# Four 64x64 tiles a slot, and an output projection in two pieces, in an attention and feed-forward kernel

## The chip, the core and the metric

The kernel runs on one core of one Trainium2 chip. The metric is the device time of one execution in microseconds (us); smaller is better. The time before is a median over three runs.

## What is computed

Inputs are q, k, v of shape (8 batches, 12 heads, 448 positions, 64) and the weights of a gated feed-forward layer, model width 768, hidden width 1536. Cut to what matters:

```python
scores = np.matmul(q, k.transpose(0, 1, 3, 2)) / np.sqrt(64)
attn = np.maximum(scores, 0.0) ** 2 / 448
x = np.matmul(attn, v)              # heads side by side: (8 * 448, 768)
xn = x / np.sqrt(np.mean(x * x, axis=-1, keepdims=True) + 1e-06) * rms_g
g = xn @ w_gate
out = (g / (1 + np.exp(-g)) * (xn @ w_val)) @ w_out
```

The matrix products run in bf16 and accumulate in fp32.

## The kernel before

**Two streams of work.** Attention of batch b + 1 is laid between the feed-forward products of batch b. `attention(b)` returns a list of units. For each pair of heads `j` and each block `c` of 128 keys there is one `scores` unit (line 212): two matmuls, one per head of the pair, each with 64 rows of contraction (the head size) and 128 output columns. `rectify` (lines 200, 202 and 205) takes the maximum with zero on ScalarE or VectorE into an SBUF tile `r`, and VectorE squares it. `attend` (line 258) multiplies the squares with v: seven groups of four matmuls with 64 rows and 64 columns, and between them one group of four from `rest_scores` (line 227), for the keys that are left over. Batches 0 and 1 get their transposed q and k from TensorE (line 177), the others by DMA.

**The feed-forward products.** A `Group` is one accumulation: for gate and value 6 blocks of 128 rows into a PSUM tile `psP` of 128x448, for the output projection 12 blocks into `psO`, and `norm_sums` with 6 blocks into `psSS`, which sums the squares of x for the norm. All are issued at line 380. Every block is cut into its lower and upper 64 rows, which are the two row halves of the array. `Stream.step` fills one slot: it picks a group `lead` for the lower half and another group `follow` for the upper half, and issues one matmul of each, 64 rows by 128 columns. A group so passes the lower half first with all its blocks, and the upper half later with the same blocks.

**The rules of picking.** `pick` lets a group go on until a multiple of six blocks, then takes the first open group that is `ready`, and for the lower half a new one from the list if none is. A group may change halves only when it has rested for `APART = 2` slots. On the change, a `nop` on TensorE's queue waits for the group's last matmul in the other half. A `Piece` (a part of the output projection) stops at half of its blocks until its siblings of the same 128 tokens are there too.

**PSUM.** `ps_m` has four banks, for all groups of the stream and the transposes. A new group begins only when a bank has been read out by its consumer: `silu` on ScalarE (line 451) for the gate, `hidden` on VectorE (line 456) for the value, `store` on ScalarE (line 490) for the output, the square root on ScalarE (line 420) for the norm. `ps_s` has two double banks, for scores and attention.

**The norm.** When `psSS` of batch b + 1 is complete, ScalarE takes the square root (with a table load on either side), VectorE the reciprocal (line 424), and then six multiplications, one for each 128 columns of the model width, give `xn` (line 427). The first product of batch b + 1 waits for these.

**The order.** All is issued in the order of the program; the loop at its end spreads the attention units over the first 82% of a batch's slots by an estimated cost. Before the loop, `attention(0)`, `norm(0)` and the first three products of batch 0 run by themselves.

Of the kernel before, what the change touches and what calls it, by code (L numbers as in the profile page):

```python
# [20 lines left out]
def kernel(  # L21
# [11 lines left out]
    nc = tc.nc  # L33
    P = nc.NUM_PARTITIONS
    B, H, S, D = q.shape
    T, DM = out.shape
# [27 lines left out]
    qkT = {}  # L64
# [3 lines left out]
    def load(nm, b, h0=0, h1=H):  # L68
        runs = nm == "v" or b < PE_T
        n, w = (PC, NCH) if nm == "q" else (P, UH)  # L70
        if (nm, b) not in ld:
            shape = [n, H, w * D] if runs else [n, w, H * D]
            ld[nm, b] = ldpool.tile(shape, BF16, name=nm + "b", tag=nm + "b")
            if nm == "k" and runs:
                nc.vector.memset(ld[nm, b][D:, :, (UH - 1) * D :], 0.0)
        t = ld[nm, b]
        src = src_of[nm][b, h0:h1]
        if nm == "q":
            parts = [(slice(0, PC), PC, 0, NCH)]
        else:  # L80
            parts = [(slice(0, D), D, 0, UH), (slice(D, P), D, UH if nm == "k" else UH - 1, U)]
        for prt, n, u0, u1 in parts:
            if runs:
                nc.gpsimd.dma_start(  # L84
                    out=t[prt, h0:h1, : (u1 - u0) * D],
                    in_=src.rearrange("h (p u) d -> p h (u d)", p=n)[:, :, u0 * D : u1 * D],
                )
            else:
                to = t[prt].rearrange("p u (h d) -> p u h d", d=D)
                rows = src.rearrange("h (p u) d -> p u h d", p=n)  # L90
                step = u1 - u0 if nm == "q" else 1
                for u in range(u0, u1, step):
                    nc.gpsimd.dma_start(  # L93
                        out=to[:, u - u0 : u - u0 + step, h0:h1, :], in_=rows[:, u : u + step]
                    )
# [4 lines left out]
    def transpose_dma(b):  # L100
        new_qkT(b)
        for c in range(UH):
            n = P if c < UH - 1 else D
            nc.sync.dma_start_transpose(
                out=qkT[b][:, :, 0, c * P : c * P + n], in_=ld["k", b][:n, c, :]
            )
        for c in range(NCH):
            nc.sync.dma_start_transpose(
                out=qkT[b][:, :, 1, c * PC : (c + 1) * PC], in_=ld["q", b][:, c, :]
            )  # L110
# [55 lines left out]
    behind = mybir.DependencyInfo(mybir.DependencyClass.Sync, mybir.DependencyReason.DATA)  # L166
# [30 lines left out]
    def rectify(b, j, c, psS):  # L197
        r = apool.tile([P, 2, S], BF16, name="r", tag="r")
        if relu_on(b, j, c) == "dve":
            nc.vector.tensor_relu(out=r[:], in_=psS[:, :, :S])  # L200
        else:
            nc.scalar.activation(out=r[:], in_=psS[:, :, :S], func=ACT.Relu)  # L202
        eng = nc.gpsimd if square_on(b, j, c) == "pool" else nc.vector
        flush()
        pending.append(lambda: eng.tensor_tensor(out=r[:], in0=r[:], in1=r[:], op=ALU.mult))  # L205
        rsq[b, j, c] = r

    def scores(b, j, c):
        psS = ps_s.tile([P, 2, 512], FP32, name="psS", tag="psS")
        for hh in range(2):  # L210
            prt = slice(hh * D, (hh + 1) * D)
            nc.tensor.matmul(  # L212
                out=psS[:, hh, :S],
                lhsT=qkT[b][prt, j, 0, c * P : (c + 1) * P],
                rhs=qkT[b][prt, j, 1, :],
                start=True,
                stop=True,
            )
        rectify(b, j, c, psS)

    def rest_scores(b, j):
# [59 lines left out]
    def attention(b):  # L281
        units = []

        def add(cost, *fns):
            units.append((cost, lambda: [f() for f in fns]))

        if b < PE_T:
            add(0.4, lambda: transposes(b, 0))
            add(0.4, lambda: transposes(b, 1))
            add(0.3, lambda: rectify(b, 0, UH - 1, rest_scores(b, 0)))  # L290
        for j in range(HP):
            for c in range(UH - 1):
                if c == 2 and j in (2, 4):
                    add(1.6, lambda j=j: attend(b, j - 2, (b, j)))
                add(0.3, lambda j=j, c=c: scores(b, j, c))
                if c == 1 and b < PE_T and j + 2 < HP:
                    add(0.4, lambda j=j: transposes(b, j + 2))
                if b == 0:
                    add(0.3, lambda: keep_busy(1))
        add(0.1, flush)  # L300
        add(1.6, lambda: attend(b, HP - 2, (b + 1, 0) if PE_T <= b + 1 < B else None), flush)
        return units
# [3 lines left out]
    class Stream:  # L306
# [28 lines left out]
        def step(self):  # L335
            if not (self.todo or self.open):
                return False
            lead = self.pick(0, None)
            follow = self.pick(1, lead)
            for half, g in ((0, lead), (1, follow)):  # L340
                if g is not None:
                    g.emit(half)
            self.at = [lead, follow]
            for g in self.open:
                g.rest += 1
            if follow is not None and follow.count[1] == follow.n:
                self.open.remove(follow)
                follow.done(follow.ps)
            return True
# [7 lines left out]
    class Group:  # L357
# [14 lines left out]
        def begin(self):  # L372
            self.ps = ps_m.tile([P, 512], FP32, name=self.name, tag="mm")

        def emit(self, half):
            i = self.count[half]
            prt = slice(half * D, (half + 1) * D)
            if self.last not in (None, half):
                tc.add_manual_dep(nc.tensor.nop().ins, self.mm.name, behind)
            mm = nc.tensor.matmul(  # L380
                out=self.ps[:, : self.w], lhsT=self.lhsT(i)[prt], rhs=self.rhs(i)[prt],
                start=(half == 0 and i == 0), stop=(half == 1 and i == self.n - 1),
            )
            self.count[half] += 1
            self.last, self.rest = half, 0
            self.mm = mm.ins

    class Piece(Group):

# [81 lines left out]

    osts = {}

    OW = DM // 3

    def outproj(i, t):
        trio = []
        for o in range(0, DM, OW):
            Piece(
                trio, FT, OW, lambda fk: hTs[i][:, fk, t * P : (t + 1) * P],  # L480
                lambda fk, o=o: wo_sb[:, fk, o : o + OW],
                lambda ps, o=o: store(i, t, o, OW, ps), "psO",
            )
        return trio

    def store(i, t, o, w, ps):
        if (i, t) not in osts:
            osts[i, t] = [opool.tile([P, DM], FP32, name="ost", tag="ost"), 0]
        ost = osts[i, t][0]
        nc.scalar.copy(out=ost[:, o : o + w], in_=ps[:, :w])  # L490
        osts[i, t][1] += w
        if osts[i, t][1] == DM:
            g, end = t * P, (t + 1) * P
            while g < end:
                n = min(end, (g // PC + 1) * PC) - g
                b, c, p0 = 2 * i + g // S, g % S // PC, g % PC
                rows = out[b * S : (b + 1) * S, :].rearrange("(p u) m -> p u m", u=NCH)
                nc.sync.dma_start(
                    out=rows[p0 : p0 + n, c, :], in_=ost[g - t * P : g - t * P + n, :]
                )  # L500
                g += n
# [21 lines left out]
    for b in range(B):  # L523
# [9 lines left out]
        if b + 2 < B:  # L533
            for nm in ("q", "k", "v"):
                load(nm, b + 2)
            side.insert(len(side) // 2, (0, lambda b=b: transpose_dma(b + 2)))
        cost = {KT: S / 2.4 + 2.5, FT: OW / 2.4 + 2.5}
        total = sum(g.n * cost[g.n] for g in groups)
# [41 lines left out]
```

## Time and profile before

| | |
|---|---|
| median of three runs | 468.2 us (466.82, 468.2, 469.97) |
| span of the profiled execution | 466.5 us, 12798 instructions |
| the profiled execution's own time | given by the page as its span alone |
| TensorE matmul busy | 453.6 us, 97% of the span, 5722 matmuls |
| TensorE weight load busy | 292.8 us, 63% |
| VectorE busy | 274.0 us, 59% |
| ScalarE busy | 234.9 us, 50% |
| GpSimd busy | 80.6 us, 17% |
| mean granted TensorE clock | 0.982 |

Engines are named PE (TensorE matmul), PEld (TensorE weight load), DVE (VectorE), ACT (ScalarE) and POOL (GpSimd). A group line of the page reads: line of the kernel, engine, operation, output <- inputs, rows*columns of the array tile and shapes, count, then busy time and mean duration of one in ns. A timeline line reads: start in us, length in us, engine, line, operation, shapes, count; matmuls that overlap are merged into one line. "64*128" is an array tile of 64 rows and 128 columns. A matmul's duration goes from its first column to its last result, and the next one on the same tile starts before that; the pace is read from starts.

### The profile page before, as it was taken

What the parts mean: (1) busy time and instruction counts of PE and PEld (TensorE: products, weight loads), DVE (VectorE), ACT (ScalarE), POOL (GpSimd) and SP (SyncE); (2) the same over time, 40 slices, a digit from 0 to 9 for tenths busy, and PEclk for the clock granted to TensorE, in tenths of its full rate; (3) what the DMA queues carried; (4) which work ended last, traced back from release to release, by engine and by line L of the source; (5) the groups of instructions that cost most, each with busy time, mean ns of one, the idle gap of its engine ahead of it and who ended that gap; (6) DMA issues with size and microseconds to landing.
All of it is one profiled execution on the core that took longest, in us unless ns stands there. A gap on an engine that the chain in (4) does not pass through costs nothing.

```text
span 466.5 us, 12798 instructions
## 1 busy us (share of the span) xinstructions
PE 453.6 (97%) x5722; PEld 292.8 (63%) x5722; DVE 274.0 (59%) x403; ACT 234.9 (50%) x360; POOL 80.6 (17%) x97
## 2 busy tenths in 40 slices
PE   6989999999999999999999999999999999999995
PEld 3434655676666766676666766676667766676674
DVE  1676378866663867576566657576656677332200
ACT  1682246665645655375445755465535764532221
POOL 8438211571007000340007000100000000000000
PEclk8698999999999999999999999999999999999998
DMA  9999999799907970299209960438002200020013
GB/s 106 194 204 199 206 173 162 80 204 165 127 3 107 214 124 2 23 200 146 44 1 124 211 109 1 58 82 135 20 1 54 85 2 1 2 84 20 1 42 95
DMA packets 130758, 44.47 MB, mean 95 GB/s; under 512 B 102928, under 2 KB 127120, under 8 KB 130704
## 3 DMA queue, kind: packets, MB, share of 16 engines
q0 software_dynamic: 91648, 24.39, 54.1%
q1 hardware_dynamic: 39056, 19.28, 20.5%
q8 instruction: 44, 0.72, 0.6%
q14 instruction: 10, 0.08, 0.0%
HBM read 48.76 MB, written 11.01 MB: 128 GB/s over the span
## 4 chain that ended last, share of the span: by engine, by line
PE 91%; DVE 3%; ACT 2%; DMA 1%; POOL 1%; issue 1%; POOLq 0%
PE psP L380 47%; PE psO L380 23%; PE psAV L258 8%; PE psS L212 6%; PE psSS L380 2%; ACT r L202 2%; PE psB L140 1%; PE psT L177 1%; PE psS L227 1%; DMA kb<-in_k_dram 1%; DVE xn L427 1%; PE psP L441 1%; DVE r L200 1%; DVE r L205 1%; DVE rstd L424 1%
## 5 line engine op out<-in xcount | busy, mean ns | idle before, releaser
L380 PE MATMUL psP<-xn,wv_sb 64*128 64x448 bf16 x1140 | 229.0, 349 | 0.0
L380 PE MATMUL psP<-xn,wg_sb 64*128 64x448 bf16 x1128 | 227.8, 349 | 0.1
L380 PE MATMUL psO<-wo_sb,hT 64*128 64x256 bf16 x2016 | 139.6, 271 | 0.0
L202 ACT ACTIVATE r<-psS 128x896 bf16<-128x896 f32 x123 | 111.1, 918 | 47.5 <-PE psS L212 46.8
L380 PEld LDWEIGHTS <-wv_sb 64*128 64x128 bf16 x1140 | 96.1, 94 | 41.5 <-issue 4.3
L380 PEld LDWEIGHTS <-hT 64*128 64x128 bf16 x2016 | 101.1, 94 | 33.0 <-issue 2.9
L380 PEld LDWEIGHTS <-wg_sb 64*128 64x128 bf16 x1128 | 94.3, 94 | 35.6 <-issue 1.3
L205 DVE TENSOR_TENSOR r<-r 128x896 bf16<-128x896 bf16 x165 | 100.9, 628 | 16.3 <-ACT r L202 15.6
L456 DVE TENSOR_TENSOR hT<-sil,psP 128x448 bf16<-128x448 bf16 x96 | 59.5, 620 | 79.7 <-PE psP L380 52.4
L451 ACT ACTIVATE sil<-psP 128x448 bf16<-128x448 f32 x96 | 51.9, 542 | 74.7 <-PE psP L380 68.8
L200 DVE TENSOR_SCALAR r<-psS 128x896 bf16<-128x896 f32 x45 | 49.1, 1090 | 31.7 <-PE psS L227 24.2
L212 PE MATMUL psS<-qkT 64*128 64x448 bf16 x288 | 59.3, 358 | 1.9 <-DVE r L200 1.2
L490 ACT COPY ost<-psO 128x256 f32<-128x256 f32 x84 | 30.5, 372 | 43.5 <-PE psO L380 39.6
L276 ACT ACTIVATE xT<-psAV 128x896 bf16<-128x896 f32 x24 | 22.0, 917 | 54.4 <-PE psAV L258 50.1
L258 PE MATMUL psAV<-r,vb 64*64 64x448 bf16 x672 | 43.9, 361 | 1.8 <-POOL r L205 1.2
L84 POOL DMA_DIRECT2D vb<-in_v_dram x18 | 13.2, 750 | 167.7 <-PE psO L380 122.3
L424 DVE RECIPROCAL rstd<-rstd 128x448 f32<-128x448 f32 x8 | 23.6, 2953 | 26.0 <-ACT rstd L420 26.0
L93 POOL DMA_DIRECT2D kb<-in_k_dram x42 | 33.0, 1008 | 18.7 <-DMA wo_sb<-in_moe_w_out_dram 9.6
L258 PEld LDWEIGHTS <-vb 64*64 64x64 bf16 x672 | 17.3, 106 | 22.3 <-issue 10.3
L427 DVE SCALAR_TENSOR_TENSOR xn<-xT,g_sb,rstd 128x448 bf16<-128x448 bf16 x48 | 29.3, 680 | 0.3
L212 PEld LDWEIGHTS <-qkT 64*128 64x128 bf16 x288 | 19.8, 94 | 11.4 <-issue 6.2
L140 PE MATMUL psB<-busy_bf,ones_bf 128*128 128x448 bf16 x58 | 17.6, 418 | 1.3 <-DVE busy_bf L135 1.3
(38 smaller groups left out, 161.7 us busy)
## 6 DMA issues: line engine op xcount, KB each, us to landing
vb<-in_v_dram POOLq DMA_DIRECT2D x14, 384.0 KB, 7.2
qb<-in_q_dram POOLq DMA_DIRECT2D x7, 672.0 KB, 12.9
kb<-in_k_dram POOLq DMA_DIRECT2D x43, 96.0 KB, 12.7
out_dram<-ost SPq DMA_DIRECT2D x8, 336.0 KB, 4.1
wg_sb<-in_moe_w_gate_dram POOLq DMA_DIRECT2D x4, 576.0 KB, 16.5
wv_sb<-in_moe_w_val_dram POOLq DMA_DIRECT2D x4, 576.0 KB, 18.1
wo_sb<-in_moe_w_out_dram POOLq DMA_DIRECT2D x2, 1152.0 KB, 21.4
out_dram<-ost SPq DMA_DIRECT2D x8, 288.0 KB, 4.4
```

Source lines behind the costliest of these rows:

```text
L93: nc.gpsimd.dma_start(out=to[:, u - u0 : u - u0 + step, h0:h1, :], in_=rows[:, u : u + step])
L200: nc.vector.tensor_relu(out=r[:], in_=psS[:, :, :S])
L202: nc.scalar.activation(out=r[:], in_=psS[:, :, :S], func=ACT.Relu)
L205: pending.append(lambda: eng.tensor_tensor(out=r[:], in0=r[:], in1=r[:], op=ALU.mult))
L212: nc.tensor.matmul(out=psS[:, hh, :S], lhsT=qkT[b][prt, j, 0, c * P : (c + 1) * P], rhs=qkT[b][prt, j, 1, :], start=True, stop=True,)
L258: mm = nc.tensor.matmul(out=psAV[hh * D : (hh + 1) * D, jj, :S], lhsT=v[prt, 2 * (j + jj) + hh, u * D : (u + 1) * D], rhs=r[prt, hh, :], s ...
L380: mm = nc.tensor.matmul(out=self.ps[:, : self.w], lhsT=self.lhsT(i)[prt], rhs=self.rhs(i)[prt], start=(half == 0 and i == 0), stop=(half = ...
L424: nc.vector.reciprocal(out=rstd[:], in_=rstd[:])
L427: nc.vector.scalar_tensor_tensor(out=xn[:, kt, :], in0=xTs[b][:, kt, :], scalar=g_sb[:, kt : kt + 1], in1=rstd[:], op0=ALU.mult, op1=ALU.mult,
L451: nc.scalar.activation(out=s[:], in_=psG[:], func=ACT.Silu)
L456: nc.vector.tensor_tensor(out=hTs[b // 2][:, fb, o : o + S], in0=sil[b, fb][:], in1=psV[:], op=ALU.mult)
L490: nc.scalar.copy(out=ost[:, o : o + w], in_=ps[:, :w])
```

## The change

Scores, gate, value, output projection and the norm's sums behind the first norm are each issued as matmuls of 64 rows by 64 columns instead of 64 by 128. A slot then holds four matmuls: lead and follow for output columns 0 to 63, then lead and follow for columns 64 to 127. The waits for a change of halves, `ordered`, now stand ahead of all four. The output projection goes from three pieces of 256 columns to two of 384.

```diff
+    quarters = [True]
+    def blocks():
+        return ((0, D), (D, P)) if quarters[0] else ((0, P),)
+
     def scores(b, j, c):
         psS = ps_s.tile([P, 2, 512], FP32, name="psS", tag="psS")
-        for hh in range(2):
-            prt = slice(hh * D, (hh + 1) * D)
-            nc.tensor.matmul(
-                out=psS[:, hh, :S],
-                lhsT=qkT[b][prt, j, 0, c * P : (c + 1) * P],
+        for m0, m1 in blocks():
+            for hh in range(2):
+                prt = slice(hh * D, (hh + 1) * D)
+                nc.tensor.matmul(
+                    out=psS[m0:m1, hh, :S],
+                    lhsT=qkT[b][prt, j, 0, c * P + m0 : c * P + m1],
...
             follow = self.pick(1, lead)
-            for half, g in ((0, lead), (1, follow)):
-                if g is not None:
-                    g.emit(half)
+            pair = [(half, g) for half, g in ((0, lead), (1, follow)) if g is not None]
+            quarters[0] = True
+            for half, g in pair:
+                g.ordered(half)
+            for m in blocks():
+                for half, g in pair:
+                    g.emit(half, *m)
+            for half, g in pair:
+                g.emitted(half)
...
+        def ordered(self, half):
+            if self.last not in (None, half):
+                tc.add_manual_dep(nc.tensor.nop().ins, self.mm.name, behind)
+
-        def emit(self, half):
+        def emit(self, half, m0, m1):
             i = self.count[half]
             prt = slice(half * D, (half + 1) * D)
-            if self.last not in (None, half):
-                tc.add_manual_dep(nc.tensor.nop().ins, self.mm.name, behind)
             mm = nc.tensor.matmul(
-                out=self.ps[:, : self.w], lhsT=self.lhsT(i)[prt], rhs=self.rhs(i)[prt],
+                out=self.ps[m0:m1, : self.w], lhsT=self.lhsT(i)[prt, m0:m1],
+                rhs=self.rhs(i)[prt],
                 start=(half == 0 and i == 0), stop=(half == 1 and i == self.n - 1),
             )
+            self.mm = mm.ins
+
+        def emitted(self, half):
             self.count[half] += 1
             self.last, self.rest = half, 0
-            self.mm = mm.ins
...
-    OW = DM // 3
+    OW = DM // 2
```

More of the change, by code (lines that the diff above doesn't have):

```diff
@@ L206, in rectify @@
         rsq[b, j, c] = r
+    quarters = [True]
+    def blocks():
+        return ((0, D), (D, P)) if quarters[0] else ((0, P),)
     def scores(b, j, c):
         psS = ps_s.tile([P, 2, 512], FP32, name="psS", tag="psS")
-        for hh in range(2):
-            prt = slice(hh * D, (hh + 1) * D)
-            nc.tensor.matmul(
-                out=psS[:, hh, :S],
-                lhsT=qkT[b][prt, j, 0, c * P : (c + 1) * P],
[L215 to L218, printed above, removed]
+        for m0, m1 in blocks():
[4 more added lines that the diff above has]
+                    lhsT=qkT[b][prt, j, 0, c * P + m0 : c * P + m1],
+                    rhs=qkT[b][prt, j, 1, :],
+                    start=True,
+                    stop=True,
+                )
         rectify(b, j, c, psS)
```

## The prediction

> **What bounds the kernel now.** I read the page's busy times first, then its groups, then the list of TensorE's waits, and last the timeline of single engines.
>
> ```profile
> PE 453.6 (97%) x5722; PEld 292.8 (63%) x5722; DVE 274.0 (59%) x403; ACT 234.9 (50%) x360; POOL 80.6 (17%) x97
> ...
> L380 PE MATMUL psP<-xn,wv_sb 64*128 64x448 bf16 x1140 | 229.0, 349 | 0.0
> L380 PE MATMUL psP<-xn,wg_sb 64*128 64x448 bf16 x1128 | 227.8, 349 | 0.1
> L380 PE MATMUL psO<-wo_sb,hT 64*128 64x256 bf16 x2016 | 139.6, 271 | 0.0
> ```
>
> TensorE is full. From starts in the timeline (445.23 and on for psO, 218.80 and on for psP) a slot of two 448-column matmuls takes 0.189 us and one of two 256-column matmuls 0.109 us. That is a fixed price per column, 0.080 us for 192 columns, and 2.6 ns a slot. The next list holds every wait of TensorE on another engine.
>
> ```profile
> PE psT L177 <- DMA kb<-in_k_dram: 2.4, 1, 2.4
> PE psB L140 <- DVE busy_bf L135: 1.3, 1, 1.3
> PE psS L212 <- DVE r L200: 1.2, 3, 0.5
> PE psAV L258 <- POOL r L205: 1.2, 1, 1.2
> PE psS L227 <- DVE qkT L182: 0.2, 1, 0.2
> PE psAV L258 <- DVE r L205: 0.2, 1, 0.2
> ```
>
> Not one is for a bank of `psP` or `psO`: PSUM is read out in time everywhere. Next is the neighbourhood of one `attend`.
>
> ```profile
> 216.54 0.35 PE L380 MATMUL psP<-xn,wv_sb 64*128 64x448 bf16 x1
> ...
> 216.86 0.95 PE L258 MATMUL psAV<-r,vb 64*64 64x448 bf16 x16
> 217.64 0.36 PE L227 MATMUL psS<-qkT 64*64 64x448 bf16 x4
> 217.88 0.79 PE L258 MATMUL psAV<-r,vb 64*64 64x448 bf16 x12
> 218.60 0.36 PE L380 MATMUL psP<-xn,wv_sb 64*128 64x448 bf16 x1
> ...
> 218.80 0.35 PE L380 MATMUL psP<-xn,wv_sb 64*128 64x448 bf16 x1
> ```
>
> Eight slots of four 64x64 matmuls run at the same 0.189 us as a slot of two. What is lost lies at the borders between tile shapes: 0.32 us from the last product to the first psAV (0.13 too many), 0.78 for the first four slots (0.02 too many), 0.72 for the last three (0.15 too many, 0.02 of it after the wait in the middle), 0.20 for the first product (0.01).
>
> **Part 1, the streaming.** Half the output columns in twice the matmuls stream the same columns: 0.189 us a slot as in the attend above. The output projection goes from 28 x 3 x 12 = 1008 slots of 0.1093 to 28 x 2 x 12 = 672 of 0.1627 (448 and 256 columns interpolated; bounds are those two, 0.189 and 0.109): 110.2 to 109.3 us, **-0.9 us**.
>
> The weight loads change from 94 ns (64x128, page) to 102 to 107 ns (64x64, the loads of line 258), four a slot; there they start 3 ns apart and lie side by side, under the slot before. I cost them at nothing. Were that cover gone, one load of 107 ns in a slot, the rest beside it, would still be under 0.163.
>
> [...]
>
> **Part 2, the borders.** Products, scores and attention now share one tile shape, so 0.13 + 0.02 + 0.13 + 0.01 = 0.29 us go at each of the 21 attends beside products (batches 1 to 7): **-6.2 us** (bounds 0 and -6.5). The transposes of line 177 keep their own shape, and so do the matmuls between the scores of batch 0: no change there.
>
> **Part 3, the change of halves.** The waiting `nop` moves ahead of the lead's matmuls, so what is queued behind it is the whole slot. A 384-column matmul should be over 0.322 us after its start (269 and 349 ns interpolated), and the wait in the attend above ended 0.07 us after that (the fourth psAV slot starts at 216.86 + 0.02 + 3 x 0.189 = 217.45; with 0.35 it is over at 217.80, and the next psAV starts at 217.88): 0.39 us, where two slots give 0.325. Each such change costs 0.07, and 0.02 for loads not fetched ahead. Walking the rules of picking through the whole list of groups, I count 71 changes in the output projection at two slots' distance: 71 x 0.1 = 7 us. Before, the last stretch of psO (chain of waits: 16.26 us for 279 matmuls, 0.115 a slot without the last one's tail) shows 6 ns a slot over 0.109: 1008 x 6 ns = 6 us for the same thing. **+1 us** (bounds -6 and +7). A product's change costs nothing where it comes later than two slots, which is part 4.
>
> **Part 4, the banks.** This decides. The walk gives, with three pieces, two open groups in the product phase: the follow is one group behind the lead. With two pieces neither may be resumed when the last tile's second piece has done its lower half, so the lead opens the next batch's first product while both pieces still owe 18 half slots. From batch 1 on the follow is then two groups behind, three groups are open, and as both halves move one block a slot this never heals. The fourth bank must be read out five slots after its group's last slot, where before there were eleven: counted from the start of the group's last matmul, 6 x 0.189 = 1.135 us instead of 12 x 0.189 = 2.27 us. The readout, undisturbed:
>
> ```profile
> 443.77 0.35 PE L380 MATMUL psP<-xn,wg_sb 64*128 64x448 bf16 x1
> 444.15 0.54 ACT L451 ACTIVATE sil<-psP 128x448 bf16<-128x448 f32 x1 [1.73 <-PE psP L380]
> 444.52 0.73 PE L380 MATMUL psP<-xn,wv_sb 64*128 64x448 bf16 x3
> 445.36 0.62 DVE L456 TENSOR_TENSOR hT<-sil,psP 128x448 bf16<-128x448 bf16 x1 [1.65 <-PE psP L380]
> ```
>
> A gate group's last matmul starts at 443.77 and ScalarE is through at 0.93 later; the value group's last of three starts at 444.90 and VectorE is through 1.08 later. TensorE goes on 0.05 after that (the psS that waited for DVE r). So 0.98 and 1.13 us against 1.135: on time by nothing, and any other work in the queue ahead (0.92 for a ScalarE r, 1.09 and 0.63 for VectorE's) is a wait of the whole array. I paired the 94 gate and 95 value readouts of the trace with their last matmuls: 22 and 20 end beyond 1.135 us, by 6.3 and 7.4 us together; none beyond 2.27. Seven of eight batches: 12 us. Against it, an attention unit between gives some slots more (0.19 or 1.5 us); for it, a wait sets the readouts into a phase in which VectorE is 70% busy (24.16 of 34.5 us in the stretch 156.5 to 191), and the next come late too. I take **+17 us** (bounds 4 and 27). The output pieces hold three or four banks also: a value readout that stands behind the norm's 6.6 us on VectorE can hold up one: **+2 us** (0 to 5). The wider copy, between 0.372 and 0.543 us, is nearer 0.49, and 56 of it are less than 84 of 0.372: free.
>
> **Part 5, the norm.** The next batch's first product now starts while more of the output projection is open, so sooner after `psSS`.
>
> ```profile
> 148.40 0.73 PE L380 MATMUL psSS<-x,ones_bf 64*128 64x448 bf16 x3
> ...
> 150.26 2.95 DVE L424 RECIPROCAL rstd<-rstd 128x448 f32<-128x448 f32 x1 [5.56 <-ACT rstd L420]
> 153.25 3.66 DVE L427 SCALAR_TENSOR_TENSOR xn<-xT,g_sb,rstd 128x448 bf16<-128x448 bf16 x6
> ...
> 156.53 0.35 PE L380 MATMUL psP<-xn,wg_sb 64*128 64x448 bf16 x1
> ```
>
> From the last psSS (148.78) the sixth xn takes 8.1 us; the product's sixth block needs it 0.95 us after its start, so a start before 7.2 us waits. Before, batches 1, 2 and 3 start at 6.4 (with a wait), 7.75 and 7.9, the others at 11 or more. By the walk the three start 2.0 to 2.6 us sooner, so they wait 2.8 + 2.0 + 1.8: **+7 us** (bounds 2 and 9); the others keep some 1 us or more.
>
> **Sum.** -0.9 - 6.2 + 1 + 17 + 2 + 7 = +19.9 us. The profiled execution's span, 466.5 us, would become 486.4; the median of the runs is 1.7 above that span, so 468.2 + 19.9 = **488 us**.
>
> **Rivals.** (a) The readouts keep up: ScalarE is 50% and VectorE 59% busy, and attention units fall into the five slots. Without part 4 the norm's wait stays: 468.2 - 6.1 + 7 = 469 us. For it: mean load; against it: 42 late readouts in the trace. (b) The walk is wrong on the lag, and neither banks nor norm cost anything: 468.2 - 6.1 = 462 us, faster. (c) Slower by another mechanism: TensorE cannot feed eight instructions a slot for long. The attends show eight slots, no more; the longest stretch of the shortest slot, psO, shows four instructions in 0.109 us, 27 ns each. If that were the floor, slots would take 0.219 us: 1176 x 0.030 + 672 x 0.056 = 73 us, 541 us. It decides as soon as an instruction needs over 20 ns; against it, psO's pace follows its columns, so 27 ns is only an upper bound.
>
> **Chances.** The forecast 0.77, with 474 to 503 for its own range by the bounds of part 4 and 5; (a) 0.11; (b) 0.08; (c) 0.04. A measurement of this kernel tells about 1% from no change: (b) is faster, (a) the same, the rest slower. The range takes in (a) and leaves out (b) and (c): 468 to 503.
>
> **What would show it.** Right: TensorE waits for hT L456's and sil L451's counterparts before psP, some 40 times, 15 us or more; waits for xn at three batch borders; 0.19 us at the borders of attend; psO x2688 of some 0.32 us. Wrong: no waits before psP and a busy share still at 97% (a or b), or slots of 0.2 us and more inside a run of products (c). If the waits are there but attend's borders still cost 0.3 us, part 2 fell.

## The result, and the profile after

| | before | after |
|---|---|---|
| median of the runs of this comparison | 467.5 us (466.5 to 470.0, 4 runs) | 497.2 us (494.6 to 497.5, 4 runs) |
| ratio to before, 95% interval | | 1.0607 (1.0567 to 1.0647) |
| profiled execution: own time, span | span 466.5 us | 497.1 us, span 495.3 us |
| mean granted TensorE clock | 0.982 | 0.980 |

The change costs 29.7 us, by the spans 28.8 us. Forecast were 19.9 us. The granted clock is the same, so the time went into waits and pace. From the page after, its head and the group of the output projection:

```profile
PE 460.8 (93%) x9034; PEld 309.7 (63%) x9034; DVE 273.0 (55%) x403; ACT 233.6 (47%) x332; POOL 80.6 (16%) x97
...
L394 PE MATMUL psO<-wo_sb,hT 64*64 64x384 bf16 x2688 | 156.3, 330 | 5.5 <-DVE hT L473 5.5
```

The output projection has its 2688 matmuls of 0.33 us, the new tiles are there. TensorE is busy for 93% instead of 97%; the three other engines do what they did. The waits of TensorE on other engines (engine, output and line, what it waited for: us in all, times, longest) show the new ones at the head of the list:

```profile
PE psP L394 <- DVE hT L473: 7.8, 14, 1.1
PE psO L394 <- DVE hT L473: 5.5, 3, 5.0
PE psP L394 <- DVE xn L444: 3.0, 14, 0.3
...
PE psP L394 <- ACT sil L468: 1.0, 4, 0.3
```

**This list shows less than a wait costs.** Its idle time starts at the modelled end of the matmul before, 0.35 us after that one's start, while the next slot was due 0.19 us after it: 0.16 us of every wait is not in the list, and a wait below that isn't there at all. So I took the loss from starts: each slot's start, subtracted from the next one's, less the slot's pace (0.189 us for 448 columns, 0.163 for 384, 0.109 for 256), summed by what the late slot had to wait for, in both traces, from the first product (48.9 and 48.6 us) to the last matmul (461.2 and 489.9 us):

| where the time stands | before | after | difference | forecast |
|---|---|---|---|---|
| all slots of the stream at their own pace (part 1) | 340.8 | 337.4 | -3.5 | -0.9 |
| slots behind or in an attend (part 2) | 9.1 | 2.2 | -6.9 | -6.2 |
| changes of halves within two slots, and slots with no cause (part 3) | 2.4 | 8.9 | +6.5 | +1 |
| first slots of a group, waiting for a bank (part 4) | 0 | 18.3 | +18.3 | +17 |
| one output block behind the norm (part 4's last piece) | 0 | 5.2 | +5.2 | +2 |
| first product waiting for xn (part 5) | 0 | 6.2 | +6.2 | +7 |
| stalls that no semaphore explains, four | 0 | 3.6 | +3.6 | 0 |

With the transposes (-0.3) the differences make 29.1 us, against 28.8 by the spans. (The first slots of groups came 1.7 us early in all before; that is pace and stands in the 2.4. The first row also holds that fewer slots mix two widths.)

**A bank that is read out late**, with VectorE's queue beside TensorE's (in brackets the idle time before and what ended it):

```profile
240.56 1.09 DVE L200 TENSOR_SCALAR r<-psS 128x896 bf16<-128x896 f32 x1 [1.04 <-PE psS L218]
240.70 1.14 PE L394 MATMUL psP<-xn,wg_sb 64*64 64x448 bf16 x20
...
241.57 0.61 DVE L205 TENSOR_TENSOR r<-r 128x896 bf16<-128x896 bf16 x1
242.10 0.61 DVE L473 TENSOR_TENSOR hT<-sil,psP 128x448 bf16<-128x448 bf16 x1
...
242.77 0.35 PE L394 MATMUL psP<-xn,wv_sb 64*64 64x448 bf16 x1 [0.93 <-DVE hT L473]
```

Twenty matmuls are five slots, so the next was due at 240.70 + 5 x 0.189 = 241.65. It starts at 242.77, 1.12 us late, of which the list shows 0.93. The readout that it needs (line 473) stood on VectorE behind a maximum and a square for the next attention: it ended at 242.71. In all, 39 first slots of a `psP` group come more than 0.06 us late, by 17.3 us (one of them, 0.8 us, is a stall without a semaphore); 13 of the 39 are late by less than 0.16 us and so leave no idle time.

**The norm's wait**, at the start of batch 3:

```profile
217.78 0.34 PE L394 MATMUL psP<-xn,wg_sb 64*64 64x448 bf16 x1 [0.16 <-DVE xn L444]
217.78 0.35 PE L394 MATMUL psO<-wo_sb,hT 64*64 64x384 bf16 x1
...
218.37 0.35 PE L394 MATMUL psP<-xn,wg_sb 64*64 64x448 bf16 x1 [0.21 <-DVE xn L444]
218.37 0.35 PE L394 MATMUL psO<-wo_sb,hT 64*64 64x384 bf16 x1
```

The product moves one block each 0.60 us, the pace of the six multiplications of line 444 (3.66 us for six), and the output projection's matmul in the other half, which has all it needs, moves no sooner. This happens at the borders of batches 1, 2 and 3 only.

**One block of 5 us**, at the end of batch 6 (counted from 0), behind the norm of batch 7:

```profile
424.73 2.95 DVE L441 RECIPROCAL rstd<-rstd 128x448 f32<-128x448 f32 x1 [1.15 <-ACT rstd L437]
...
426.15 0.84 PE L394 MATMUL psO<-wo_sb,hT 64*64 64x384 bf16 x16
427.79 3.66 DVE L444 SCALAR_TENSOR_TENSOR xn<-xT,g_sb,rstd 128x448 bf16<-128x448 bf16 x6
431.37 0.61 DVE L473 TENSOR_TENSOR hT<-sil,psP 128x448 bf16<-128x448 bf16 x1
432.03 0.85 PE L394 MATMUL psO<-wo_sb,hT 64*64 64x384 bf16 x8 [5.04 <-DVE hT L473]
```

The output projection needs the last `hT` of its batch as data, and VectorE makes it only behind the reciprocal and six multiplications of the norm. From the slot due the block comes 5.2 us late.

**What became better** is the border of attend:

```profile
285.85 0.79 PE L264 MATMUL psAV<-r,vb 64*64 64x448 bf16 x12
286.44 0.58 PE L394 MATMUL psP<-xn,wv_sb 64*64 64x448 bf16 x8
```

Three slots of psAV take 0.59 us to the product's first matmul, 0.57 by the pace; before they took 0.72.

### The profile page after: what moved, and what is told of

Its sections match the earlier page's. It is cut to its first block, busy times and chain, and to the rows that moved or that the text cites. A ratio compares the mean times of both kernels' runs of the same rounds, so it can differ in the third digit from the quotient of the medians.

```text
span 495.3 us, 19394 instructions
## 1 busy us (share of the span) xinstructions
PE 460.8 (93%) x9034; PEld 309.7 (63%) x9034; DVE 273.0 (55%) x403; ACT 233.6 (47%) x332; POOL 80.6 (16%) x97
## 4 chain that ended last, share of the span: by engine, by line
PE 75%; DVE 14%; ACT 4%; issue 4%; POOL 1%; DMA 1%; DVEq 0%; ACTq 0%; POOLq 0%
PE psP L394 38%; PE psO L394 19%; PE psAV L264 7%; PE psS L218 5%; DVE r L200 4%; DVE xn L444 3%; DVE r L205 2%; DVE rstd L441 2%; DVE hT L473 2%; PE psSS L394 2%; PE psB L140 1%; ACT r L202 1%; PE psT L177 1%; PE psS L233 1%; DMA kb<-in_k_dram 1%
## 5 line engine op out<-in xcount | busy, mean ns | idle before, releaser
L394 PE MATMUL psP<-xn,wv_sb 64*64 64x448 bf16 x2280 | 176.6, 351 | 8.0 <-DVE hT L473 7.8
L394 PE MATMUL psP<-xn,wg_sb 64*64 64x448 bf16 x2256 | 178.1, 351 | 5.5 <-DVE xn L444 3.0
L394 PE MATMUL psO<-wo_sb,hT 64*64 64x384 bf16 x2688 | 156.3, 330 | 5.5 <-DVE hT L473 5.5
L394 PEld LDWEIGHTS <-hT 64*64 64x64 bf16 x2688 | 94.2, 108 | 52.7 <-PE psO L394 16.1
L394 PEld LDWEIGHTS <-wg_sb 64*64 64x64 bf16 x2256 | 98.0, 107 | 44.5 <-issue 15.9
L394 PEld LDWEIGHTS <-wv_sb 64*64 64x64 bf16 x2280 | 98.6, 107 | 29.8 <-issue 3.9
L205 DVE TENSOR_TENSOR r<-r 128x896 bf16<-128x896 bf16 x165 | 101.6, 628 | 16.7 <-ACT r L202 15.7
L218 PE MATMUL psS<-qkT 64*64 64x448 bf16 x576 | 58.1, 359 | 2.9 <-DVE r L200 1.6
L507 ACT COPY ost<-psO 128x384 f32<-128x384 f32 x56 | 26.6, 478 | 55.7 <-PE psO L394 55.5
L218 PEld LDWEIGHTS <-qkT 64*64 64x64 bf16 x576 | 21.8, 107 | 12.3 <-issue 6.8
L394 PE MATMUL psSS<-x,ones_bf 64*64 64x448 bf16 x168 | 19.0, 351 | 0.2 <-DVE x L284 0.2
```

The source lines that it names most:

```text
L218: nc.tensor.matmul(out=psS[m0:m1, hh, :S], lhsT=qkT[b][prt, j, 0, c * P + m0 : c * P + m1], rhs=qkT[b][prt, j, 1, :], start=True, stop=True,)
L394: mm = nc.tensor.matmul(out=self.ps[m0:m1, : self.w], lhsT=self.lhsT(i)[prt, m0:m1], rhs=self.rhs(i)[prt], start=(half == 0 and i == 0), s ...
```

## The experiments

All ratios are to the kernel before, run beside each.

### Which part of the change costs what

**e1_tiling_alone**: the 64x64 tiles, with the output projection in three pieces as before.

```diff
-    OW = DM // 2
+    OW = DM // 3
```

> Four 64x64 tiles a slot, but three pieces of 256 columns as before. Lag theory (the two pieces leave a third group open; the banks, the norm and the last hidden block then come late): the lag stays one group, so no waits of psP for a bank, and the borders of attend save 6 us; but the wait for a change of halves now holds the whole slot: some 150 products at two slots' distance (0.42 needed, 0.38 there: 0.05 and 0.02 each) and 150 changes in psO (0.34 needed, 0.22 there: 0.12 each) cost 11 + 19 us less the 6 that were paid already: 485 us (480 to 490). Rival, the tiling is free and the pieces alone cost time: 468 - 6 = 462 us. Rival, the 64x64 tiles themselves starve the array: 500 us and more, with slots over 0.19 us inside a run of products.

Measured: 512.8 us, ratio 1.094 (1.091 to 1.097). But for one wait of 0.7 us behind the readout of a transpose, there is no wait for a bank, and none for xn, so the lag does come with the two pieces. But the tiling alone costs more than the whole change: by the same account 31 us in slots of the output projection and mixed slots, 7.6 us at 154 changes of halves in the products (0.05 us each), and 15 us of stalls that no semaphore explains, most of them before `psO`:

```profile
PE psO L394 <- issue: 9.0, 6, 2.9
```

"issue" is the profile's word for time in which an engine waited for nothing that it shows. This was in none of my theories. The time is that of the second rival (500 us and more), but not for its reason: inside a run of products a slot still takes 0.19 us (starts at 299.66, 299.85 and 300.04).

**e2_pieces_alone**: the kernel before, with two pieces.

```diff
-    OW = DM // 3
+    OW = DM // 2
```

> 64x128 tiles as before, but two pieces of 384 columns. Lag theory: all of the loss is here: psP waits for banks 17 us, the norm 7, the last hidden block 5 to 8, less 1 to 3 us of slots saved: 496 us (490 to 502), the same as the whole change, because the borders saved and the costlier change of halves balance there. Rival, the pieces are harmless or better and the tiling costs the time: 468 us or less, and no psP wait for hT or sil.

Measured: 491.0 us, ratio 1.0486 (1.0465 to 1.0507).

```profile
PE psP L380 <- DVE hT L456: 7.5, 14, 1.0
PE psO L380 <- DVE hT L456: 5.7, 3, 5.1
PE psP L380 <- DVE xn L427: 3.9, 15, 0.5
```

With 64x128 tiles the three waits of the change appear nearly number for number (bank starts 16.7 us by the account), and no issue stall. The pieces alone give 22.7 of the 29.7 us. The two costs don't add: two pieces cure much of what the tiles cost with three, since a slot of 384 columns (0.163 us) leaves a change of halves more time than one of 256 (0.109), and there are fewer of them. In the order in which the kernels issue their matmuls, some 360 changes come within two slots in e1 and 96 in the change: with the follow two groups behind, most changes of a product come later, so the lag that makes banks late also hides changes.

### Is the lag the cause, and does the wait's place matter?

**e3_own_wait**: the wait for a change of halves stands ahead of the two matmuls of its own group, not of all four.

```diff
-            for half, g in pair:
-                g.ordered(half)
-            for m in blocks():
-                for half, g in pair:
+            for half, g in pair:
+                g.ordered(half)
+                for m in blocks():
                     g.emit(half, *m)
```

> The changed kernel, but each group's wait for its change of halves stands directly ahead of that group's own two matmuls, as before the change, so that the lead's matmuls are not held by the follow's wait. Lag theory with the wait's place as a smaller term: the 71 changes of psO at two slots' distance cost 0.1 us less each in part, 4 us in all: 493 us (489 to 496). Rival, the place of the wait is the main cost: 475 us or less. Rival, it costs nothing: 497 us.

Measured: 493.6 us (490.0 to 495.7), ratio 1.0532 (1.0472 to 1.0592). By the medians some 3.7 us come back, as expected, but the interval overlaps that of the change (1.0567 to 1.0647), and the profiled execution's span, 493.9 us, is 1.4 us below the change's. With two pieces the place of the wait costs little; that it costs anything is not shown by this run.

**e7_three_own**: the same edit on e1.

> Four tiles a slot, three pieces of 256 (as the tiling alone, 512.8 us), but each group's wait stands directly ahead of its own two matmuls. Theory: the place of the wait costs the tiling alone some 21 us (154 products and some 190 changes in psO and mixed slots, 0.05 to 0.14 us each), since here the lead goes on while the follow waits: 492 us (486 to 498). What is left over the kernel before would be the feeding of TensorE with instructions (profile: waits put down to issue). Rival, the feeding is the main loss and the place of the wait a small one: 505 us or more, with the waits at issue as they were.

Measured: 495.4 us, ratio 1.059 (1.0554 to 1.0625). With three pieces the place of the wait is worth 17.4 us. The slots there are 0.109 us, two of them 0.219, against an estimated 0.34 us until a wait on a 256-column matmul is through (0.271 by the page before and the 0.07 of the attend in part 3): a wait ahead of all four holds up the other half as well.

**e4_lag_cured**: the rest is set for each kind of group, three slots for products and one for output pieces, so that the pieces may be resumed when the lead looks for work.

```diff
-            if self.last not in (None, half) and self.rest < stream.APART:
+            if self.last not in (None, half) and self.rest < self.APART:
```

> The changed kernel, but a piece may change halves after one slot and a product after three. Walking the rules of picking, the follow is then one group behind again in the product phase. Lag theory: the waits of psP for banks and for xn go (-24 us), while the change of halves in psO at one slot's distance costs 7 us more: 476 us (470 to 483). Rival, late readouts come from ScalarE's and VectorE's load and not from the lag: waits of psP for hT stay at 10 us and more, and the time rises by those 7 us to 504 us.

Measured: 487.0 us, ratio 1.0393 (1.0362 to 1.0423). I expected 476.

```profile
PE psO L395 <- DVE hT L474: 4.4, 3, 4.0
```

The issue stalls are 5.8 us (3.3 before `psP`, 1.5 before `psO`, 1.0 before `psS`). The waits of `psP` for hT fall from 14 to 1 (0.2 us; a transpose waits once, 0.5 us), those for sil and for xn are gone: one rule of picking makes both, so the lag is their cause. Only 10 of some 24 us come back. Of the 19 us over before, the block behind the norm is 4.4 and the issue stalls are 5.8. Most of the rest is the change of halves: a piece may make it here after one slot, where the wait (about 0.39 us by the estimate in part 3) outlasts the slot (0.163). By the starts in this trace 56 such changes are late by 14.8 us in all, 0.26 each, against 8.5 us for the 96 of the change and 2.4 us in the kernel before; the borders of attend give some 6 us back. About 2 us stay open.

**e5_no_squares**: the squaring of `r` is left out in batches 1 to 7, so VectorE has less ahead of its readouts.

```diff
-        pending.append(lambda: eng.tensor_tensor(out=r[:], in0=r[:], in1=r[:], op=ALU.mult))
+        if b == 0:
+            pending.append(lambda: eng.tensor_tensor(out=r[:], in0=r[:], in1=r[:], op=ALU.mult))
```

> The changed kernel without the squaring of r in batches 1 to 7 (left out; attention then uses the rectified scores themselves): 138 operations of 0.63 us less on VectorE. Theory: readouts late in the queue are what TensorE waits for in the product phase; about half of those waits go, 10 to 13 us: 485 us (481 to 490), psP waits for hT at half. Rival, VectorE's load does not matter, the readout's own length does: 495 us or more, waits as they were.

Measured: 490.3 us, ratio 1.0489 (1.0455 to 1.0523), 7 us less than the change; expected was 485. The waits of `psP` for hT fall from 7.8 us in 14 to 2.7 in 5, those for ScalarE's `sil` do not (1.0 us in 4, now 1.4 in 5). So the queue ahead of the readout is what makes a bank late, and five slots still leave some late without the squares.

**e6_old_xn**: the products of batch b read the xn of batch b - 1, which has long been there (two buffers of xn, two of the output stage to make room). The norm is computed, its result used a batch later.

> The changed kernel, but the products of batch b read the xn of batch b - 1 (so the output is of other values; the norm and its six multiplications are all still done; xn has two buffers and the output stage two instead of three). Theory: the waits of psP for xn go, 6.6 us by the trace: 490 us (487 to 493). Rival, what is saved there is given back at the next bank: 497 us.

Measured: 496.4 us (495.0 to 498.8), ratio 1.0625 (1.0579 to 1.0671): no gain. All waits for xn are gone, the waits for banks are the same (7.8 us in 14), and issue stalls rise from 0.9 us in one to 4.9 us in three before `psP`.

Six us of waits are taken away, and nothing comes back at the end. The stalls take most of it back (4.9 against 0.9 us in the list); the rest is not taken apart. The time is that of the rival, 497 us, but its reason, that the next bank takes it back, does not show: counted from starts too, the first slots of `psP` are late by some 17 us in both traces.

### What the tiling itself costs

**e8_three_own_apart3**: e7 with a rest of three slots for all groups, so that a change of halves should be hidden.

> As the run with three pieces and each group's own wait, and a group rests three slots, not two, before it changes halves. Theory: the wait of a product's change is then over before it is met; 3 to 4 us less than that run: 488 us, and if the feeding with instructions cost nothing this version would beat the kernel before by the 6 us of the borders, at 461 us. Rival, rest of three slots opens a third group, with waits of psP for banks: 500 us or more.

Measured: 489.2 us, ratio 1.0464 (1.0423 to 1.0504), as expected. Neither banks, xn nor halves are left as a cost here; what is left is this:

```profile
PE psO L394 <- issue: 14.8, 6, 3.1
```

Eight stalls of 1.1 to 3.4 us from the slot due, 20.3 us together. One of them in the timeline, and the stretches of 2 us around it (length, then busy time and count of PE, PEld, DVE, ACT and POOL, granted clock, DMA share, GB/s):

```profile
267.67 4.11 POOL L93 DMA_DIRECT2D kb<-in_k_dram  x5
268.33 1.15 PE L394 MATMUL psO<-wo_sb,hT 64*64 64x256 bf16 x34
...
272.27 0.96 PE L394 MATMUL psO<-wo_sb,hT 64*64 64x256 bf16 x28 [2.79 <-issue]
```

```profile
268.00:270.00 2.00, 1.48 (x56) 1.27 (x47) 2.00 (x1) 1.23 (x4) 2.00 (x5) 1.00 1.20 209
270.00:272.00 2.00, 0.00 (x0) 0.00 (x0) 1.96 (x5) 0.00 (x0) 1.78 (x3) 1.00 1.93 211
```

For two whole microseconds no matmul and no weight load starts, at a granted clock of 1.00, while the inputs of a later batch come in at 210 GB/s. The trace also has transfers of a queue named "instruction": 81 of 16 KB in this kernel, 44 before. TensorE's 2 x 10378 matmuls and weight loads, by 81, are 256 instructions to a transfer (2 x 5722 by 44 are 260): it used one up in some 11 us before, and in 4 to 6 us here. The fetch in this stall started at 270.08, 0.9 us after TensorE had stopped; the one before it at 261.5. The stalls stand at the borders of such blocks: between the ends of two neighbouring stalls (159.86 and 166.61, 212.50 and 219.52, 272.28 and 279.02 us) the trace has 128 matmuls and 128 weight loads each time, 256 together, and between those at 102.16 and 122.66 it has 768. All eight end 2.2 to 2.8 us after the start of a 16 KB transfer. These eight transfers took 0.9 to 1.3 us, like the others of their queue (0.9 to 1.4), so it is their start that is late rather than that they take long. My reading: they stood behind the input loads. In the kernel before, with its 44 transfers, the list of TensorE's waits has no issue wait.

**e10_no_late_loads**: e8, with the loads of q, k and v for batches 4 to 7 left out (these batches compute on older inputs).

> The version with three pieces, own waits and three slots of rest (489.2 us), with the loads of q, k and v for batches 4 to 7 left out (they are computed from the loads of batches 2 and 3). That version's trace has eight stalls of 1.1 to 3.4 us in which TensorE waits for no semaphore, each around a late fetch of 16 KB of instructions: four of them (98.8, 121.3, 157.7, 163.4 us) beside the loads for batches 2 and 3, four (211.2, 215.9, 269.2, 275.7 us) beside those left out here, 10.8 us together, and none after the loads end. Theory, the fetch stands behind the input loads: the late four go and the early four stay, 478 us (475 to 482). Rival, TensorE's rate of instructions is itself over what a fetch can bring: all stay, 489 us.

Measured: 470.9 us (467.2 to 472.5), ratio 1.0049 (1.0025 to 1.0073); I expected 478. The loads are the cause of the stalls beside them: of the stalls of 1.1 us and more two are left instead of eight (idle for 1.8 us up to 93.0 us and for 2.1 us up to 100.5 us). The miss is in my list of which loads stand where: GpSimd issues its loads as soon as its own queue lets it, ahead of the loop, so that in e8 the burst at 149 to 159 us is already v of batch 4 with q and k of batch 5, and more stalls stood beside left-out loads than I had counted. What stays (5.4 us in five before `psO` in the list) stands up to 105.3 us, beside loads that are still made, but for 0.5 us at 365 us. The trace has 81 transfers of 16 KB as in e8, so the number of instructions by itself does not make the stalls.

**e11_paced_loads**: e8 with all loads, but each cut into parts (q 4, k 7, v 3; a part of v is two transfers); a part is laid with an attention unit, behind a `nop` on GpSimd that waits for the last matmul that the stream has issued. The transposing transfers move to three quarters of the batch.

```diff
+    def pace():
+        tc.add_manual_dep(nc.gpsimd.nop().ins, stream.mm.name, behind)
...
-            for nm in ("q", "k", "v"):
-                load(nm, b + 2)
-            side.insert(len(side) // 2, (0, lambda b=b: transpose_dma(b + 2)))
+            side.insert(n * 3 // 4, (0, lambda b=b: transpose_dma(b + 2)))
+            for x, p in enumerate(parts):
+                at = 1 + x * n * 5 // 8 // len(parts)
+                ...
```

> The same version with all loads, but those for batches 2 to 7 in smaller parts, each laid with an attention unit and issued only when the last matmul before it is done, so that they spread over some 30 us of a batch and not in one burst; the transposing transfers move from the middle to three quarters of the batch's units. Theory: fetches get through between the parts; most of the 20 us of stalls go: 471 us (465 to 478). Rival, a fetch waits behind any part as long as behind the burst: 485 us or more.

Measured: 464.0 us (462.4 to 465.6), ratio 0.9904 (0.9876 to 0.9932), 25 us less than e8, and faster than both kernels of this study, if by 1% only against the kernel before. Nothing is left out here; the bytes are the same, only spread. Of the issue stalls little stays (1.4 us in one before `psO`, 1.1 in two before `psP`). So TensorE was fed eight instructions a slot here, where the loads don't come in one burst.

**e9_before_apart3**: the kernel before with a rest of three slots.

> The kernel before, with three slots of rest instead of two before a change of halves. Theory: what the changes in the output projection cost there (my part 3 put it at 6 us, the trace's sum of late slots at about 2 us) goes for the most part: 466 us, 2 us less (0 to 4). Rival, a third group opens and banks come late: 475 us or more.

Measured: 464.4 us (463.4 to 465.4), ratio 0.9912 (0.9893 to 0.9932). The kernel before can have 4 us by this alone, and its span, 461.6 us, is that of e11. With everything cured that these runs found, the 64x64 tiles are thus worth no more than the 64x128 ones, within these intervals; the kernel before with paced loads as well was not run.

**e12_after_paced**: the changed kernel with paced loads.

> The changed kernel (497.2 us) with the loads for batches 2 to 7 spread in the same way. Theory: its trace has about 3 us in which TensorE waits for no semaphore beside late fetches of instructions (121.9, 277.7, 72.8, 90.1 us), hidden otherwise by the waits for banks; these go, 494 us (491 to 496). Rival, the feeding is what my sum was short of altogether: 487 us. Rival, what is saved is given back at the next bank, as it was with the norm: 497 us.

Measured: 490.8 us (488.6 to 494.7), ratio 1.0481 (1.044 to 1.0521), some 6 us less than the change. The issue waits are gone from the list of TensorE's waits, but so are 3.1 us of waits for banks (7.8 in 14 to 4.7 in 9), probably because the moved transposes shift the attention units; the block behind the norm and the waits for xn stay to the tenth. The profiled execution was the slowest of the six, its span only 2.4 us below the change's. So the run is no clean measure of the stalls: it does not contradict the 3.6 us of the account, and does not confirm them.

## Why the prediction was right, and where it fell short

The direction, the range and the place of the loss were right; 10 us of the size were missing. Some of the closeness is luck: parts 1 and 2 came out 3 us better than forecast, without which the miss would be 13. Two figures of the working do not come out as written: 21 attends at 0.29 us are 6.1 us, not 6.2, and the lower bounds of parts 4 and 5 give 468 us, not 474.

**Part 1** held: a slot of four tiles keeps the pace of its columns (0.19 us for 448 in e1, 0.163 for 384 in the change), and no cost of the weight loads, 106 to 107 ns each, shows even with 10378 of them (e11, 464 us). Rival (c) as I wrote it, a floor of 27 ns an instruction, is ended too: in e8 slots of `psO`, eight instructions each, start 0.109 us apart (268.93, 269.04, 269.15 us).

**Part 2** held: -6.9 against -6.2.

**Part 3** is the first term that failed. The price of a change was right (8.5 us at 96 changes within two slots, 0.09 each; I had 0.1 for 71, so the count was short), but I set against it 6 us already paid before, by spreading the pace of the last stretch of psO over all 1008 slots. The account of the trace before finds 2.4 us in that row. By starts, undisturbed stretches of psO in both halves lie 3 to 4 ns a slot over the pace, not 6 (from 143.0 to 146.4 us 0.1127 us a slot), and the one that I spread has a single jump of 0.12 us at its start. 5 us of the 10 are this.

**Part 4** held in mechanism and size: 18.3 us against 17, some 39 late starts against "some 40"; e2 shows them without the tiling, e4 takes them away with the lag, e5 a good part of them with VectorE's queue. What I said would show it, "TensorE waits ... 15 us or more" in the list, does not show there, since the list has 8.8 us; it shows in the starts. Its last piece, a readout behind the norm at +2, was 5.2. It was also not a bank: it is the output projection waiting for hT as data, so the whole of the norm's 6.6 us on VectorE lies on the path, less what TensorE still had to do. My own upper bound of 5 was the better value.

**Part 5** held: 6.2 against 7, at the three borders named. But e6 shows that taking this wait away alone brings nothing, so a term of the account is not what its removal gives.

**The instruction feed**, costed at nothing, is 3.6 us in the change and 20 in e8. I had asked only whether TensorE can take so many instructions, not whether they arrive. The three issue waits in the list of the change (0.9, 0.7 and 0.5 us) also end 2.5 to 3.2 us after the start of a 16 KB transfer. Rival (c) was the right question in the wrong form.

## What to carry to other kernels

When the number of pieces or the rest of a software pipeline changes, walk through the order of picking and count how many slots remain between a group's end and the next use of its bank; compare that with the readout *and* the queue ahead of it, not with the engine's mean load. A wait put ahead of a whole slot also held what was ready (17.4 us, e1 against e7). Before doubling the instructions of an engine, look at the instruction queue's transfers and at the bursts of input beside them; spreading the loads gave more here (25 us, e8 to e11, though only some 6 us in the changed kernel, e12) than any rearrangement of the matmuls.

## What was not expected of the hardware

- **Instructions came late.** With some 256 TensorE instructions used in 4 to 6 us, stalls of 1.1 to 3.4 us came beside input bursts of about 210 GB/s; with the loads left out (e10) two of eight stayed, with the loads spread (e11) 2.5 us of issue waits. That it is the 16 KB fetch which is late rests on the 256 instructions between neighbouring stalls, on the transfer that starts 2.2 to 2.8 us ahead of each stall's end, and on e10 and e11. What holds the transfer back was not seen.
- **One row half ran ahead of the other.** In the trace before, `psO` matmuls of 256 columns start every 0.109 to 0.119 us in the one half while `psP` matmuls of 448 columns start every 0.19 to 0.22 us in the other:

```profile
297.61 0.27 PE L380 MATMUL psO<-wo_sb,hT 64*128 64x256 bf16 x1
297.61 0.35 PE L380 MATMUL psP<-xn,wg_sb 64*128 64x448 bf16 x1
297.72 0.27 PE L380 MATMUL psO<-wo_sb,hT 64*128 64x256 bf16 x1
297.83 0.36 PE L380 MATMUL psP<-xn,wv_sb 64*128 64x448 bf16 x1
297.83 0.39 PE L380 MATMUL psO<-wo_sb,hT 64*128 64x256 bf16 x2
298.03 0.35 PE L380 MATMUL psP<-xn,wv_sb 64*128 64x448 bf16 x1
298.06 0.38 PE L380 MATMUL psO<-wo_sb,hT 64*128 64x256 bf16 x2
298.22 0.35 PE L380 MATMUL psP<-xn,wv_sb 64*128 64x448 bf16 x1
298.28 0.38 PE L380 MATMUL psO<-wo_sb,hT 64*128 64x256 bf16 x2
298.41 0.54 PE L380 MATMUL psP<-xn,wv_sb 64*128 64x448 bf16 x2
```

  The kernel issues one matmul of each to a slot, yet the eighth `psO` starts at 298.39 us and the fifth `psP` at 298.41, so one half runs ahead of the order of issue here. A wait still held both: in the lines of the xn wait above, `psO` stands behind a waiting `psP` in the order of issue and starts with it (217.78 and 218.37 us). Elsewhere the halves run apart in the change too (from 424.75 to 425.56 us `psO` starts every 0.16 us and `psP` every 0.19).
